# A gated mix of two linear-attention blocks: output tiles as pairs with seven block products, denominators on TensorE, and queries as a filling stream

## The chip, the cores and the metric

The kernel runs on one core of a Trainium2 chip. A core has TensorE (PE in the profile: matmuls, into PSUM, which has 8 banks of 512 fp32 for each of 128 partitions), VectorE (DVE), ScalarE (ACT), GpSimd (POOL), and SyncE (SP), which here only issues DMAs. The metric is the device time of one execution in microseconds. Less is better.

## The reference

x is 2048 x 640 in bf16. Two blocks, A and B, with weights of their own read the same x (B's own x isn't used), and a gate mixes their outputs:

```python
x = A_x
g = sigmoid((x * gate_w).sum(-1, keepdims=True))
a = block(x, A_wqkv, A_wo)
b = block(x, B_wqkv, B_wo)
return g * a + (1 - g) * b

def block(x, wqkv, wo):                          # S=2048, D=640, H=32 heads of 20
    q, k, v = split_heads(x @ wqkv)
    phi = lambda t: where(t > 0, t + 1, exp(t)) + 1e-6
    pq, pk = phi(q), phi(k)
    kv = einsum("bhsd,bhse->bhde", pk, v)
    z = einsum("bhsd->bhd", pk)
    num = einsum("bhqd,bhde->bhqe", pq, kv)
    den = einsum("bhqd,bhd->bhq", pq, z)[..., None] + 1e-6
    return merge_heads(num / den) @ wo
```

## The kernel before

**The plan.** The kernel makes a list of operations, each with engine, estimated cost, buffers read and written, and a priority. `Sched.run` (L111) goes through it with the estimated costs and fixes an order for every engine and a slot for every pooled buffer (PSUM banks, staging slots); `Sched.emit` (L214) writes each engine's program in that order, with semaphore waits between engines. TensorE takes its operations strictly as listed (`look = cand[:1]`, L148); other engines take what can start first and, among ready operations, the lowest `prio`. Nearly all DMAs are issued from SP in the planned order, so one that waits for its data holds up the ones behind it.

**The stages on TensorE.** A token is a row of x. There are 16 token tiles of 128 (`NT`) in 4 blocks of 512 (`NB`), and 5 chunks of 128 features (`NC`).

1. Start: loads, warm-up matmuls (`warm`, L516), and the transposes of the first tiles (`x_tp`).
2. Keys (`k_step`, L585): for each tile and block X, five pairs of matmuls, 512 and 128 wide. `k_post` turns k into pk = phi(k) on ScalarE and VectorE. An extra column of B's weights gives the gate's sum; GE is exp of its negative. While this runs, `s_pair` and `t_all` build differences of pk and of x on VectorE.
3. pk^T x (`g_unit`, L863, five times): the 2 x 2 block product of two feature groups of pk with x is formed from seven block products, P1 to P7 in `prod` (L848), each of 8 matmuls with 320 or 321 moving columns, instead of eight. Partial results go from PSUM to SBUF (`save`, L880, ScalarE), are accumulated further in the same bank, and are added on VectorE (`comb`, L883). The 321st column sums pk over the tokens; `zsum` (L894) writes it as one column of ZC. A DMA transpose turns each result into GS.
4. Queries (`q_unit`, L786): 40 slots (2 blocks X x 4 token blocks x 5 groups) of five 512-wide matmuls; phi is two activations on ScalarE (L818, L820) and two operations on VectorE (L823, L830). 28 of them are placed between the products of pk^T x (`QPRE`, `QFILL`, called by `fill_g`), first all of A's, then B's; the other 12 follow (`QTAIL`, `POST`).
5. `kv_unit` (L951) multiplies GS by the value weights and masks the heads' diagonal blocks; `wp_burst` (L1000) folds the result into the output weights, 15 matmuls in four quadrants of the array for each half of the columns. The result WP goes to DRAM and is read back in another layout.
6. Denominators: for each X and token block, `t_sum` (L1058) sums z * pq over the five feature groups (one activation at L1078, four operations at L1076); `den` (L1086) transposes the sum by DMA, adds four partial sums per head (L1094), takes the reciprocal (L1101), multiplies it by the gate (L1108 or L1118), transposes back by DMA, and scales pq with it in two halves (L1134).
7. Outputs (`out_unit`, L1189; `o_mm`, L1144): for each of 16 tiles, five groups of A and five of B accumulate in one pair of PSUM banks:

```python
a[:, l0 - lo : h0 - lo],
PQ[X, b][:, g, 128 * (t % 4) : 128 * (t % 4) + 128],
WP[X][:, g, l0:h0],
```

with the columns as 512 and 128. `o_post` (L1170) copies 640 columns to bf16 on ScalarE and a DMA stores the tile. The first four tiles' A parts are done early (`o_a`); the last tile is stored in two parts.

Of the kernel before, what the change touches and what calls it, by code (L numbers as in the profile page):

```python
# [30 lines left out]
def _consts():  # L31
    p = np.arange(128)[:, None]
    q, m = p % 64, np.arange(24)[None, :]
    bd = np.where(p < 64, (q >= 4) & ((q - 4) // 20 == m // 4), (q < 60) & (3 + q // 20 == m // 4))
    be = q // 20 == m[:, 0:8] // 4
    return _bf16_bits(np.concatenate([bd, be], axis=1).astype(np.float32))


CW = 32
# [8 lines left out]
TSACT = [(X, b) for X in XS for b in range(4)]  # L48
WPDVE = (("B", 0, 1), ("B", 1, 1))
QR = "ACT"  # L50
QFILL = ((3, 1, 1, 1), (2, 1, 1, 1), (2, 1, 1, 1), (2, 1, 1, 1), (2, 1, 1, 1))
QTAIL = ((1, [8, 9]), (2, [5]), (2, [6, 7]), (2, [8, 9]), (3, [5, 6]), (3, [7, 8]), (3, [9]))
WOAT = (3, 0)
POST = ("q", "q", "kv", "q", "0", "q", "1", "den", "a", "q", "q", "q")
OAN = 4
STACT = (("B", 0),)
PR = {("B", 0): -0.5, ("A", 2): 10**5, ("A", 3): 10**5 + 1}
FFACT = (("B", 1), ("B", 2), ("B", 3), ("A", 2), ("A", 3))
KVAT = (3, 0)
WPAT = ((3, 1), (3, 2))  # L60
# [12 lines left out]
class Op:  # L73
    def __init__(self, eng, fn, cost, ins, outs, after, prio, name, dma):
        self.eng, self.fn, self.cost, self.ins, self.outs = eng, fn, cost, ins, outs
        self.prio, self.name, self.dma = prio, name, dma
        self.deps = list(after)
# [6 lines left out]
        for b in outs:  # L84
            b.writers.append(self)
        self.start = self.end = None
# [9 lines left out]
class Sched:  # L96
    ENGS = ("SP", "ACT", "POOL", "PE", "DVE")

    def __init__(self, pools):
        self.ops = []  # L100
        self.free = {k: [(0.0, i, []) for i in range(n)] for k, n in pools.items()}
        self.order = []

    def op(self, eng, fn, cost, ins=(), outs=(), after=(), prio=None, name="", dma=None):
        if eng == "ACT" and dma is None:
            after = list(after) + self.consts
        o = Op(eng, fn, cost, list(ins), list(outs), after, len(self.ops) if prio is None else prio, name, dma)
# [3 lines left out]
    def run(self):  # L111
# [10 lines left out]
        def can(o, t):  # L122

            w = t
            if o.behind is not None and o.behind.start is None:
                return None
            for d in o.deps:
                if d.end is None:
                    return None
                w = max(w, d.end + (HOP if d.eng != o.eng or d.dma else 0.0))  # L130
            skip = set()
            for b in o.outs:
                if b.pool and b.slot is None:
                    got = self.pick(b, w, skip)
                    if got is None:
                        return None
                    w = max(w, got[0])
                    skip |= set(range(got[1], got[1] + b.n))
            return w

        n = len(self.ops)
        while len(self.order) < n:
            best = None
            for e in self.ENGS:
# [3 lines left out]
                look = cand[:1] if e == "PE" else cand  # L148
                pick = None
                for o in look:  # L150
# [3 lines left out]
                    key = (w if w > at[e] + 1e-6 else at[e], o.prio)  # L154
                    if pick is None or key < pick[0]:
                        pick = (key, o)
                if pick and (best is None or pick[0][0] < best[0][0]):
# [3 lines left out]
            (w, _), o, e = best  # L161
# [3 lines left out]
            for b in o.outs:  # L165
                o.deps += b.war
            o.start = w
# [4 lines left out]
            else:  # L172
                o.end = at[e] = w + o.cost
                if e == "PE":
                    o.end += 160.0
            todo[e].remove(o)
            self.order.append(o)
# [106 lines left out]
def body(nc, A_x, A_wqkv, A_wo, B_x, B_wqkv, B_wo, gate_w, out, log=None):  # L284
# [17 lines left out]
    NEK, NEQ, NOS, NGT, NPT = 6, 4, 4, 4, 4  # L302
# [5 lines left out]
    ZC = sb("ZC", [128, 2 * NC], f32)  # L308
# [3 lines left out]
    GE1 = sb("GE1", [128, NT], f32)  # L312
    GG = sb("GG", [128, NB, 2, 4], f32)
# [3 lines left out]
    EPQ = sb("EPQ", [128, 1], f32)  # L317
# [7 lines left out]
    TSF = {}  # L325
    for b in range(NB):
        for X in XS:
            k = b if X == "A" or b < 2 else 0
            TSF[X, b] = (TXf[:, 1792 + 1024 * b : 2816 + 1024 * b] if X == "B" and b > 1 else WKW[:, 2560 + 1024 * k : 3584 + 1024 * k]).bitcast(f32)
    DEN = sb("DEN", [128, 1280], bf)  # L330
# [21 lines left out]
    WO["B"] = [WQ["A"][:, u, :] for u in range(NU - 1)] + [GSAf[:, 1920:2560]]  # L352
    WO5 = {"A": WOA[:, 0:5, :], "B": WQ["A"][:, :, :]}

    PQ = {("A", b): PQ0[:, NC * b : NC * b + NC, :] for b in range(2)}
    for k, o in ((("A", 2), 0), (("A", 3), SSB), (("B", 0), 2560), (("B", 1), 5120), (("B", 2), SSB + 2560), (("B", 3), 7680)):
# [9 lines left out]
    OST = PKS[:, SSB + 12288 : SSB + 12288 + NOS * D].rearrange("p (k f) -> p k f", k=NOS)  # L366
    XNf = XN[:, :, :].rearrange("p t f -> p (t f)")
    DR = {("A", b): DEN[:, :] if b % 2 == 0 else EKT[:, NPT * 644 : NPT * 644 + 1280] for b in range(NB)}
    for b in range(NB):
        DR["B", b] = XNf[:, 1280 * b : 1280 * b + 1280]  # L370
    TSH = {k: r[:, 0:512] for k, r in DR.items()}
    FF = TSH
    TTR = {k: r[:, 512:1024].rearrange("p (t n) -> p t n", t=4) for k, r in DR.items()}
    FXT = {k: r[:, 512:1024] for k, r in DR.items()}
    DNT = {k: r[:, 1024:1280].bitcast(f32) for k, r in DR.items()}

    BDM = CST[:, 0:24]
    BDE = CST[64:104, 24:32]

    sch = Sched({"ps": 8, "ek": NEK, "eq": NEQ, "os": NOS, "gt": NGT, "pt": NPT})  # L380
# [47 lines left out]
    sch.consts.append(op("POOL", lambda e: e.memset(EPQ[:, :], EPS / 4), 100.0, outs=[beps], name="epq"))  # L428
    op("ACT", lambda e: e.activation(SCR[:, :], EPSC[:, :], ACT.Exp), 1500.0, ins=[beps], outs=[bge0], prio=10**6, name="table")
# [84 lines left out]
    bw = Buf("warm", "ps")  # L514

    def warm(n, w=4):  # L516
        for i in range(n):
            op(
                "PE",
                lambda e: e.matmul(psw(bw, 128 * w), ONE[:, 0:1].to_broadcast([128, 128]), ONE[:, 0:1].to_broadcast([128, 128 * w]), start=True, stop=True),  # L520
# [800 lines left out]
```

## Time and profile before

| What | Value |
|---|---|
| Time, median of 3 runs | 184.31 us (183.83 to 184.68) |
| Span of the profiled execution, first to last instruction | 183.0 us |
| Its granted TensorE clock, mean | 1.000 |
| TensorE busy, share of the span | 98% |
| VectorE, ScalarE, GpSimd busy | 73%, 64%, 1% |
| Instructions | 3186 |
| Moved by DMA | 21.38 MB, mean 117 GB/s |

The profile gives the span of its execution and no time of its own; the runs' times lie 0.8 to 1.7 us above that span.

How to read the rows: L796 is line 796 of the kernel, out<-in gives the buffers, x10 the count. A group row has the busy time, the mean of one instruction in ns, then the idle time of the engine ahead of the group and what ended it. A stage row has the stretch, its length, then for PE, PEld, DVE, ACT and POOL the busy time and count, then the granted clock, the DMA share and GB/s. Matmuls overlap, so that the duration of one is longer than its distance to the next.

### The profile page before, as it was taken

The page shows a single profiled execution, that of the slowest core. Times are in us where ns is not written, and L with a number is a line of the kernel's source. Part 1 is how long each engine was busy: PE and PEld are TensorE (multiplying, and loading weights), DVE is VectorE, ACT ScalarE, POOL GpSimd, SP SyncE. Part 2 cuts the span into 40 slices and gives each one's busy share as a digit, 9 for nine tenths or more (in the row PEclk, how much of TensorE's full clock was granted, in tenths as well). Part 3 has the DMA queues.
Part 4 walks back from the last instruction along what each step waited for, and adds up shares of the span by engine and source line. Part 5 has one row for each costly group of instructions (what it writes and reads, how often), then busy time and mean ns, then how long its engine had stood idle before and what let it go on. Part 6 is the DMA issues. An engine that isn't in the chain of part 4 may idle for free.

```text
span 183.0 us, 3186 instructions
## 1 busy us (share of the span) xinstructions
PE 179.1 (98%) x1257; PEld 106.0 (58%) x1257; DVE 132.8 (73%) x253; ACT 117.1 (64%) x213; POOL 1.3 (1%) x13
## 2 busy tenths in 40 slices
PE   9999999999999999999999999998899999999995
PEld 4455555555565666666667666655455555555552
DVE  2276978899889893884989997799997896660000
ACT  5278888898866577657563796586689538613312
POOL 1000000000000000000000000000000000000000
PEclk9999999999999999999999999999999999999999
DMA  6979999200000089210246579651168062531122
GB/s 184 315 149 146 202 379 364 64 2 0 4 0 0 20 222 191 42 36 0 39 93 151 99 147 306 212 104 29 29 181 211 0 201 65 133 102 59 49 75 72
DMA packets 36501, 21.38 MB, mean 117 GB/s; under 512 B 25694, under 2 KB 36230, under 8 KB 36486
## 3 DMA queue, kind: packets, MB, share of 16 engines
q1 hardware_dynamic: 35858, 20.59, 44.8%
q10 hardware_dynamic: 628, 0.58, 1.2%
q8 instruction: 10, 0.16, 0.4%
q14 instruction: 5, 0.04, 0.1%
HBM read 10.87 MB, written 4.26 MB: 83 GB/s over the span
## 4 chain that ended last, share of the span: by engine, by line
PE 77%; DVE 13%; DMA 7%; ACT 2%; issue 1%; SPq 0%; DVEq 0%; ACTq 0%
PE ps L591 19%; PE ps L853 18%; PE ps L1152 18%; PE ps L796 15%; PE ps L592 5%; DMA XN<-XN 3%; DMA WKW<-in_A_wqkv_dram 2%; DVE TX L1076 2%; DMA DEN<-DEN 2%; DVE WKW L1076 2%; DVE PKS L830 1%; ACT EQ L818 1%; DVE PKS L959 1%; DVE XN L1101 1%; PE ps L979 1%
## 5 line engine op out<-in xcount | busy, mean ns | idle before, releaser
L591 PE MATMUL ps<-WKW,XT 128*128 128x512 bf16 x160 | 44.6, 384 | 0.2 <-DMA WKW<-in_A_wqkv_dram 0.2
L592 PE MATMUL ps<-WKW,XT 128*128 128x128 bf16 (+1 forms) x160 | 35.4, 221 | 0.0
L1152 PE MATMUL ps<-PKS 128*128 128x512 bf16 (+1 forms) x240 | 33.4, 299 | 0.3 <-DVE PKS L1134 0.3
L818 ACT ACTIVATE EQ<-ps 128x512 bf16<-128x512 f32 (+1 forms) x35 | 22.9, 657 | 16.4 <-PE ps L796 13.9
L591 PEld LDWEIGHTS ps<-WKW,XT 128*128 128x128 bf16 x160 | 15.8, 99 | 19.6 <-issue 1.0
L1152 PEld LDWEIGHTS ps<-PKS 128*128 128x128 bf16 x240 | 18.5, 98 | 14.7 <-DVE PKS L1134 0.6
L637 ACT ACTIVATE EKT<-ps 128x640 bf16<-128x640 f32 x32 | 22.3, 704 | 7.0 <-PE ps L592 6.3
L853 PE MATMUL ps<-TX,PKS 128*128 128x321 bf16 (+1 forms) x160 | 24.7, 300 | 0.0
L1176 ACT ACTIVATE PKS<-ps 128x640 bf16<-128x640 f32 (+1 forms) x16 | 11.0, 695 | 21.1 <-PE ps L1152 21.0
L796 PE MATMUL ps<-XT,WQA 128*128 128x512 bf16 x100 | 23.9, 379 | 0.0
L796 PE MATMUL ps<-XT,WQB 128*128 128x512 bf16 x100 | 23.3, 379 | 0.0
L853 PEld LDWEIGHTS ps<-TX,PKS 128*128 128x128 bf16 x160 | 15.3, 98 | 8.4 <-issue 0.4
L820 ACT ACTIVATE PKS<-ps 128x512 bf16<-128x512 f32 (+1 forms) x25 | 17.0, 680 | 1.8 <-PE ps L796 1.8
L853 PE MATMUL ps<-XN,PKS 128*128 128x321 bf16 (+1 forms) x120 | 18.0, 300 | 0.0
L796 PEld LDWEIGHTS ps<-XT,WQB 128*128 128x128 bf16 x100 | 11.5, 118 | 8.6 <-issue 0.2
L796 PEld LDWEIGHTS ps<-XT,WQA 128*128 128x128 bf16 x100 | 11.7, 117 | 8.0
L592 PEld LDWEIGHTS ps<-WKW,XT 128*128 128x128 bf16 x160 | 15.8, 99 | 0.0
L853 PEld LDWEIGHTS ps<-XN,PKS 128*128 128x128 bf16 x120 | 11.7, 98 | 5.4
L823 DVE TENSOR_SCALAR EQ<-EQ 128x512 bf16<-128x512 bf16 (+1 forms) x35 | 10.8, 308 | 5.5 <-ACT EQ L818 5.4
L650 ACT ACTIVATE PKS<-ps 128x640 bf16<-128x640 f32 x20 | 14.0, 699 | 0.0
L701 DVE TENSOR_TENSOR PKS<-PKS 128x1280 bf16<-128x1280 bf16 (+1 forms) x20 | 13.5, 686 | 0.3
L830 DVE TENSOR_TENSOR PKS<-PKS,EQ 128x512 bf16<-128x512 bf16 (+1 forms) x25 | 11.8, 474 | 1.7 <-ACT PKS L820 0.6
(86 smaller groups left out, 181.2 us busy)
## 6 DMA issues: line engine op xcount, KB each, us to landing
out_dram<-PKS SPq DMA_DIRECT2D x15, 160.0 KB, 1.8
XN<-in_A_x_dram SPq DMA_DIRECT2D x1, 2240.0 KB, 9.4
WKW<-in_A_wqkv_dram SPq DMA_DIRECT2D x5, 160.0 KB, 4.0
WKW<-in_B_wqkv_dram SPq DMA_DIRECT2D x5, 160.0 KB, 3.9
WQA<-in_A_wqkv_dram SPq DMA_DIRECT2D x1, 800.0 KB, 11.0
WQB<-in_B_wqkv_dram SPq DMA_DIRECT2D x1, 800.0 KB, 13.7
WVA<-in_A_wqkv_dram SPq DMA_DIRECT2D x1, 800.0 KB, 4.9
PKS<-in_B_wqkv_dram SPq DMA_DIRECT2D x1, 800.0 KB, 5.3
```

Of the source, the lines that this page charges most:

```text
L591: e.matmul(a[:, 0:512], l, WK[X][:, c, 0:512], start=(c == 0), stop=(c == NC - 1))
L592: return e.matmul(a[:, 512:w], l, WK[X][:, c, 512:w], start=(c == 0), stop=(c == NC - 1))
L637: op("ACT", lambda e, i=i, ps=ps: e.activation(evg(i), psg(ps), ACT.Exp), act_cost(D), ins=[ps] + first, outs=[ek, b], name="ke")
L650: op("ACT", lambda e, X=X, ps=ps: e.activation(pkt(X, t), psg(ps), ACT.Relu), act_cost(D), ins=[ps], outs=[rk], name="kr")
L701: op("DVE", lambda e: e.tensor_tensor(out=out, in0=a, in1=b, op=ALU.subtract), dve2(n * D), ins=ins, outs=[bb], name=name)
L796: r = e.matmul(PS[:, ps.slot + i, :], WQ[X][:, c, g::5], XT[:, c, 512 * b : 512 * b + 512], start=(c == 0), stop=(c == NC - 1),)
L818: op("ACT", lambda e: e.activation(ev(), pv(), ACT.Exp), act_cost(512 * n), ins=[ps], outs=[eq], name="qe")
L820: op("ACT", lambda e: e.activation(dst, pv(), ACT.Relu), act_cost(512 * n), ins=[ps], outs=[rq], after=pq_free.get((XS[slots[0] // NC], b) ...
L830: op("DVE", lambda e: e.tensor_tensor(out=dst, in0=dst, in1=ev(), op=ALU.add), dve2(512 * n), ins=[rq, eq, eq2], outs=[pq], name="qs")
L853: r = e.matmul(PS[:, ps.slot, 0:w], reg[:, j, :], mov(j, w), start=(first and j == 0), stop=(j == 7), skip_group_check=not first)
L1152: r = e.matmul(a[:, l0 - lo : h0 - lo], PQ[X, b][:, g, 128 * (t % 4) : 128 * (t % 4) + 128], WP[X][:, g, l0:h0], start=(X == "A" and g == ...
L1176: op("ACT", lambda e: e.activation(OST[:, os_.slot, 0:w], psw(ps, w), ACT.Copy), act_cost(w), ins=[ps], outs=[os_], name="oc")
```

## The change

The diff touches these places.

- **Outputs.** `o_mm`, `o_post` and `out_unit` go. `Pair` takes two neighbouring tiles: with rows [A|B] of scaled queries for two tiles and the weights WP of A over B in two column halves, their 2 x 2 block product is formed from seven products of five 320-wide matmuls each, in the manner of `g_unit`. `s_blk` builds three differences of scaled queries, and one in place, for each token block; `t_mat` builds four sums of weight halves (TO). Three evictions and one copy for each pair are on ScalarE, three additions on VectorE. Results are staged in 9 slots.
- **Denominators.** `t_sum` goes. `zsum` writes z as 32 columns, zero outside the own head (ZM). A new `den(b)` multiplies ZM with pq on TensorE, 20 matmuls of 256 columns, into four strips of 32 PSUM partitions (two X, two token halves). VectorE adds epsilon and multiplies by 1 + GE or 1 + 1/GE, transposed once by DMA (GTX; four GpSimd operations write its input); ScalarE inverts by Ln and then Exp with scale -1; four DMAs for each block copy every head's row to four partitions; scaling pq is as before. A table set with both functions is loaded ahead of the first activation.
- **Order.** Queries are marked `fill`. TensorE's list is `MAIN`: G for pk^T x, kv, w, O for pairs, den; `q34` holds the next item until 34 fills are done. Where the next item of `MAIN` would wait over 150 ns by the plan, the next fill goes ahead. Queries go by token block, A and B after one another. Three of the four dens are fills; each is queued after the first B query of the following block.
- **Rest.** The gs transposes are asked for right behind their parts; B's folded weights go out and back by halves; B's output weights load behind the last pk^T x, into the place of x; buffers get new places; warm-up matmuls go to four banks; operations on other engines are planned as overlapping by `LATE`.

```diff
+MAIN = """q2 G0.1 q5 G0.2 G0.5 G0.6 q6 G0.3 G0.7
+G1.1 G0.4 G1.2 G1.5 G1.6 G1.3 G1.7
+G2.1 G1.4 G2.2 G2.5 G2.6 G2.3 G2.7
+G3.1 G2.4 G3.2 G3.5 G3.6 G3.3 kvA G3.7
+G4.1 G3.4 G4.2 wA0 G4.5 wA1 G4.6 G4.3 G4.7 G4.4
+kvB wB0 wB1
+O0.1 O0.5 q34 O1.1 O1.5 q36 O0.2 O0.6 q38 O1.2 O1.6 q40 O0.3 O0.7 q42 O1.3 O1.7 q43 O2.1 O2.2 O0.4 O1.4 O2.5 den3 O2.6 O2.3 O2.7
+O3.1 O3.2 O2.4 O3.5 O3.6 O3.3 O3.7
+O4.1 O4.2 O3.4 O4.5 O4.6 O4.3 O4.7
+O5.1 O5.2 O4.4 O5.5 O5.6 O5.3 O5.7
+O6.1 O6.2 O5.4 O6.5 O6.6 O6.3 O6.7
+O7.1 O7.5 O6.4 O7.6 O7.2 O7.7 O7.3 O7.4"""
+SLACK = 150.0
...
+LATE = {"ACT": 110.0, "DVE": 80.0}
...
+                if e == "PE":
+                    look = [next((o for o in cand if not o.fill), None), next((o for o in cand if o.fill), None)]
+                    if look[0] is not None and look[0].needq > filled[0]:
+                        look = look[1:]
...
+                    w += SLACK if e == "PE" and o.fill and len(look) > 1 else 0.0
...
-    NEK, NEQ, NOS, NGT, NPT = 6, 4, 4, 4, 4
+    NEK, NEQ, NOS, NGT, NPT = 6, 6, 9, 4, 4
...
+        e.add_instruction(mybir.InstLoadActFuncSet(act_func_set_id=6, name=nc.get_next_instruction_name(), engine=mybir.EngineType.Activation))
+        return e.activation(SCR[:, :], EPSC[:, :], ACT.Exp)
...
-                lambda e: e.tensor_tensor(
-                    out=ZC[:, i : i + 1], in0=PS[:, ps.slot, HC : HC + 1], in1=PT[:, src.slot, HC : HC + 1], op=ALU.add
+                lambda e: e.scalar_tensor_tensor(
+                    ZM[:, i, :],
+                    PT[:, src.slot, HC : HC + 1].to_broadcast([128, 32]),
+                    PS[:, ps.slot, HC : HC + 1],
+                    HM,
+                    op0=ALU.add,
+                    op1=ALU.mult,
...
+    def den(b):
+        ps, b1, b2 = Buf("dn", "ps"), Buf("dr"), Buf("ff")
+
+        def fn(e):
+            for g in range(NC):
+                for s in range(4):
+                    i, h = s // 2, s % 2
+                    r = e.matmul(
+                        PS[32 * s : 32 * s + 32, ps.slot, 0:256],
+                        ZM[:, NC * i + g, :],
+                        PQ[XS[i], b][:, g, 256 * h : 256 * h + 256],
+                        start=(g == 0),
+                        stop=(g == NC - 1),
+                    )
+            return r
...
+            lambda e: e.scalar_tensor_tensor(DNR, PS[:, ps.slot, 0:256], EPS, gt, op0=ALU.add, op1=ALU.mult),
...
+        op("ACT", lambda e: e.activation(DNR, DNR, ACT.Ln), act_cost(256), ins=[b1], outs=[b3], prio=-1, name="ln%d" % b)
+        stt_op[b, 1] = op("ACT", lambda e: e.activation(ff, DNR, ACT.Exp, scale=-1.0), act_cost(256), ins=[b3], outs=[b2], after=fx_op.get(b - 2, []), prio=-1, name="rc%d" % b)
...
+                        bass.AP(tensor=src.tensor, offset=src.offset, ap=[src.ap[0], [0, 4], src.ap[1]]),
...
+        for k, dst, in0, in1, need in ((1, s[0], a21, a22, ()), (2, s[1], a11, s[0], (1,)), (4, s[2], a12, s[1], (2,)), (3, a21, a21, a11, (1,))):
...
+                lambda e, dst=dst, in0=in0, in1=in1: e.tensor_tensor(out=dst, in0=in0, in1=in1, op=ALU.subtract),
...
+    class Pair:
...
+                    r = e.matmul(PS[:, ps.slot, 0:HALF], reg(g), mov(g), start=(first and g == 0), stop=(g == NC - 1), skip_group_check=not first)
...
+            if n == 1:
+                self.bufa, self.bufb = [], []
+                self.mm("1", self.px, self.q("A", 0), lambda g: WP["A"][:, g, 0:HALF], True, [fa, bwpm["A", 0]])
+                self.s1 = self.save(self.t1, self.px, "o1s")
+            elif n == 2:
+                self.mm("2", self.py, self.q("B", 0), lambda g: WP["B"][:, g, 0:HALF], True, [fb, bwpm["B", 0]])
+                self.comb(self.oa, 0, self.py, self.t1, self.bufa, "o11")
+            elif n == 5:
+                self.mm("5", self.pz, self.so(0), lambda g: TO[1][:, g, :], True, [bso[b, 1], bto[1]])
+                self.s5 = self.save(self.t5, self.pz, "o5s")
+            elif n == 6:
+                self.mm("6", self.px, self.so(1), lambda g: TO[2][:, g, :], False, [bso[b, 2], bto[2]], [self.s1])
+                self.s2 = self.save(self.t2, self.px, "o2s")
+            elif n == 7:
+                self.mm("7", self.px, self.q("A", 1), lambda g: TO[3][:, g, :], False, [bso[b, 3], bto[3]], [self.s2])
+                self.c22 = self.comb(self.ob, HALF, self.px, self.t5, self.bufb, "o22")
...
+            elif n == 3:
+                self.mm("3", self.pz, self.so(2), lambda g: WP["B"][:, g, HALF:D], False, [bso[b, 4], bwpm["B", 1]], [self.s5])
+                self.comb(self.oa, HALF, self.pz, self.t2, self.bufa, "o12")
...
+            elif n == 4:
+                self.mm("4", self.px, self.q("B", 1), lambda g: TO[4][:, g, :], False, [fb, bto[4]], [self.c22])
...
+        for b, X in QORDER[2:]:
+            for k in range(NC):
+                q_unit(b, [NC * XS.index(X) + k])
+                if (X, k) == DENAT:
+                    den_s(b - 1)
```

More of the change, by code (lines that the diff above doesn't have):

```diff
@@ L176, in run @@
             todo[e].remove(o)
+            filled[0] += o.fill
             self.order.append(o)
@@ L324, in body @@
     TXf = TX[:, :, :, :].rearrange("p k j f -> p (k j f)")
[L325 to L330, printed above, removed]
+    DEN = sb("DEN", [128, 320], bf)
     EK = EKT[:, 0 : NEK * D].rearrange("p (k f) -> p k f", k=NEK)
@@ L512, in load_wo @@
             o.behind = gs_last[0]
-    bw = Buf("warm", "ps")
+    bw = Buf("warm")
     def warm(n, w=4):
@@ L1282, in body @@
+        for o in sch.ops[n0:]:
+            if o.eng == "PE" and not o.fill:
+                o.needq = need
     span = sch.run()
```

611 lines of the change are left out of this document (311 added, 300 removed).

## The prediction

> **What bounds the kernel now.** I read the page's busy times first, then its chain of work that ended last, then that chain in order of time, the stages of the span, and last the waits of TensorE. First the page, parts 1 and 4:
>
> ```profile
> PE 179.1 (98%) x1257; PEld 106.0 (58%) x1257; DVE 132.8 (73%) x253; ACT 117.1 (64%) x213; POOL 1.3 (1%) x13
> ...
> PE 77%; DVE 13%; DMA 7%; ACT 2%; issue 1%; SPq 0%; DVEq 0%; ACTq 0%
> ```
>
> TensorE is busy from end to end, so the sum is made of its instructions. A busy time counts overlapping matmuls whole; what a matmul costs in a stream is the distance between starts, and the chain in order of time has that (start us, us, what):
>
> ```profile
> 5.17 0.58 PE ps L591
> ...
> 48.62 2.16 PE ps L796 x10
> ...
> 72.72 2.20 PE ps L853 x16
> ...
> 95.60 1.43 PE ps L979 x30
> ...
> 100.33 0.53 PE ps L1013 x15
> 100.87 2.31 PE ps L853 x16
> ...
> 104.25 0.53 PE ps L1013 x15
> 104.79 1.20 PE ps L853 x8
> ...
> 149.44 31.43 PE ps L1152 x230
> 180.96 0.29 DVE PKS L1174
> ```
>
> Prices: 0.216 us for a 512-wide query matmul (L796), 2.20/16 = 0.1375 for a 321-wide one of pk^T x (L853), 31.43/115 = 0.273 for an output pair of 512 and 128. The work on TensorE: keys from 5.17 to 48.62, 43.45; queries 200 x 0.216 = 43.2; pk^T x 280 x 0.1375 = 38.5; kv 2 x 1.43 = 2.9; the folded weights 4 x 0.53 = 2.1; outputs 16 tiles x 10 pairs x 0.273 = 43.7. That is 173.85 us; from 5.17 to the last matmul's end (149.44 + 31.43 = 180.87) pass 175.70, so 1.85 us are waits. The stages and the waits of TensorE (us; line waited for, total, times, longest) say where:
>
> ```profile
> 48.50:109.20 60.70, 60.70 (x418) 38.88 (x417) 50.48 (x111) 39.75 (x75) 0.50 (x4) 1.00 0.37 75
> 109.20:149.40 40.20, 39.01 (x276) 22.60 (x274) 35.61 (x65) 27.66 (x45) 0.00 (x0) 1.00 0.53 142
> 149.40:180.90 31.50, 31.41 (x230) 17.69 (x230) 10.54 (x14) 11.93 (x24) 0.00 (x0) 1.00 0.28 86
> ...
> PE ps L1013 <- DVE PKS L959: 0.5, 1, 0.5
> PE ps L1152 <- ACT EQ L818: 0.5, 1, 0.5
> ...
> PE ps L1152 <- DVE PKS L1134: 0.3, 1, 0.3
> ```
>
> About 1.3 us of waits stand between 109 and 149.5, where kv, folded weights and denominators of the second half must come through VectorE (35.61 of 40.2 us busy). The other 0.6 us is spread and I carry it over.
>
> **The change part by part.** *Output tiles in pairs.* 16 x 10 pairs become 8 pairs x 7 products x 5 matmuls of 320 columns = 280. The width, the weights of 128 columns and the order of loads are those of L853, so 280 x 0.1375 = 38.5 for 43.7: **-5.2 us**. (At 320/512 of 0.216 it would be 37.8.)
>
> *Denominators on TensorE.* A den is 20 matmuls of 256 columns in four strips of 32 output columns. No strip over all 128 rows is in this trace; the nearest row is L1013, 15 matmuls in four quadrants. The longest quadrant has 3 of 320 columns, 0.405 us at 0.216/512 a column; the burst took 0.53, 1.31 times that. A strip has 5 x 256 columns, 0.54; by the same factor 0.71. Lower bound 0.54, upper bound all 20 in a row, 20 x 0.108 = 2.16. I take 0.71, since the burst is the only row of matmuls side by side. The group behind each burst is longer as well, 2.31 for 2.20 and 1.20 for 1.10: 0.10 for changing over, taken once per den. Four dens: 4 x 0.81 = **+3.2 us** (2.2 to 8.7).
>
> The Trainium skill, page "TensorEngine Tiling (Array Packing)", section Key Properties, says that a change of tiling mode drains TensorE, which speaks against four more changes there and back. An estimate from "TensorE: Matmul & The Clock Gate", section Single matmul latency, where a lone warm matmul costs 166 ns over its columns, is 2 x 0.17 = 0.33 a den, and the time would be 0.9 us longer than forecast. By the 0.10 behind the bursts the trace shows a smaller drain.
>
> *What leaves VectorE and ScalarE, and what comes.* Rows of the groups by shape (busy, mean ns | idle before):
>
> ```profile
> L818 ACT ACTIVATE EQ<-ps 128x512 bf16<-128x512 f32 x30 | 17.8, 596 | 13.5 <-PE ps L796 12.9 <-DVE PQ L830 0.5
> L701 DVE TENSOR_TENSOR PKS<-PKS 128x1280 bf16<-128x1280 bf16 x12 | 9.8, 820 | 0.2
> L1076 DVE SCALAR_TENSOR_TENSOR WKW<-PKS,ZC,WKW 128x512 f32<-128x512 bf16 x12 | 8.9, 749 | 0.2
> L823 DVE TENSOR_SCALAR EQ<-EQ 128x512 bf16<-128x512 bf16 x30 | 8.7, 289 | 5.5 <-ACT EQ L818 5.4
> L830 DVE TENSOR_TENSOR PKS<-PKS,EQ 128x512 bf16<-128x512 bf16 x20 | 8.4, 420 | 1.2 <-ACT PKS L820 0.3
> L886 DVE TENSOR_TENSOR WKW<-ps,EKT 128x320 bf16<-128x320 f32 x15 | 7.3, 485 | 1.8 <-PE ps L853 1.6
> L1134 DVE TENSOR_TENSOR PKS<-PKS,XN 128x1280 bf16<-128x1280 bf16 x8 | 6.2, 811 | 0.0
> L1101 DVE RECIPROCAL XN<-XN 128x128 f32<-128x128 f32 x4 | 3.8, 954 | 0.1
> L721 DVE TENSOR_TENSOR TX<-XN 128x2576 bf16<-128x2576 bf16 x2 | 3.0, 1492 | 0.0
> L959 DVE TENSOR_TENSOR PKS<-ps,CST 128x480 bf16<-128x480 f32 x2 | 2.9, 1437 | 0.0
> L1094 DVE TENSOR_REDUCE XN<-XN 128x128 f32<-128x512 bf16 x4 | 2.7, 682 | 2.9 <-DMA XN<-XN 2.9
> L1027 DVE CAST TX<-ps 124x960 bf16<-124x960 f32 x2 | 2.3, 1154 | 0.0
> L881 ACT ACTIVATE EKT<-ps 128x320 f32<-128x320 f32 x5 | 2.2, 447 | 0.0
> L429 ACT ACT_TABLE_LOAD x1 | 1.3, 1283 | 0.6 <-issue 0.6
> L1174 DVE CAST PKS<-ps 128x128 bf16<-128x128 f32 x1 | 0.3, 292 | 17.6 <-PE ps L1152 17.6
> ```
>
> From VectorE go 32 sums x 0.75 = 24.0, 8 reduces 5.5, 8 reciprocals 7.6 and 3 scalings 2.1: 39 us. To it come 24 output sums x 0.485 = 11.6, 16 differences of 1280 elements x 0.82 = 13.1, four weight sums of 1600 (between the 0.82 and 1.49 rows, by length 0.99) 3.9, four gate products under 0.485, 1.8: 30 us. So its total falls by 9 us, worth nothing while TensorE is the bound; its place matters. ScalarE gets 32 evictions x 0.447 = 14.3 and four ln and exp pairs (each under 0.447) for the 11 us of whole-tile evictions, 8 first sums and 20 scalings, hidden at 64% load. Of the DMAs, 16 transposes on SP's queue become one of the gates and 16 plain copies, so that queue is freed; nothing lands later for it. GpSimd's four gate expansions lie beside pk^T x and nothing needs them before the first den. Warm-up, constants: nothing; they end before the key matmuls or lie beside them.
>
> *Order.* Six queries (6.5 us) are due in pk^T x, which then runs without them: its end is 48.62 + 38.5 + 6.5 + 1.43 + 1.06 = 96. Behind it lie 34 queries, 36.7 us. They cover what follows: gs transpose, kv, mask, folded weights to DRAM and back, den and its ln, exp and copies, about 19 us by the same steps before (kv of A at 95.6, its folded weights asked back from DRAM at 114.61, the row below). So the 1.3 us of visible waits goes.
>
> *New waits.* In a pair the third product on one bank needs the eviction of the first, with one product (5 x 0.1375 = 0.69) in between. The timeline (start, us) has the steps:
>
> ```profile
> 113.46 1.24 PE L796 MATMUL ps<-XT,WQB 128*128 128x512 bf16 x5
> 113.66 0.44 ACT L881 ACTIVATE EKT<-ps 128x321 f32<-128x321 f32 x1 [0.67 <-PE ps L853]
> ...
> 114.61 0.43 SPq L394 DMA_DIRECT2D PKS<-wpsA  x1
> ...
> 130.23 1.02 ACT L818 ACTIVATE EQ<-ps 128x1024 bf16<-128x1024 f32 x1 [1.12 <-DVE PKS L830]
> 131.40 1.52 PE L1152 MATMUL ps<-PKS,PQ 128*128 128x512 bf16 x10 [0.48 <-ACT EQ L818]
> ```
>
> ScalarE starts 0.20 behind TensorE's switch to other work, takes 0.44, and TensorE starts 0.15 after an eviction: 0.79, so 0.10 is open, once in each of 8 pairs: 0.8. Queued behind it on TensorE is only the rest of the pair. The last pair has two more such places, 0.10 and 0.15 (sum on VectorE, 0.20 + 0.49 + 0.15): 0.25. For sums that meet a 0.82 us difference on VectorE I put 0.4 (0 to 2). With the 0.6 carried over: 2.05 for 1.85, **+0.2**. The end: a 320-wide eviction of 0.45 for 0.29, and a store of 80 KB that lies between 32 and 160 KB (landing 1.6 and 1.8 us, by the page's DMA part): **+0.25**.
>
> ```profile
> out_dram<-PKS SPq DMA_DIRECT2D x15, 160.0 KB, 1.8
> ...
> out_dram<-PKS ACTq DMA_DIRECT2D x1, 32.0 KB, 1.6
> ```
>
> Sum: -5.2 + 3.2 + 0.2 + 0.25 = **-1.55**. Span 183.0 becomes 181.45. The runs lie 0.8 to 1.7 above the span; carrying that 1.3 over to their median, 184.31 - 1.55 = **182.8**.
>
> **Rivals.** *A, VectorE takes over (slower).* From the end of pk^T x to the last query TensorE has 36.7 + three dens 2.4 + kv and folding 2.5 + twelve products 8.3 = 49.9 us. VectorE has 34 queries x 0.71 = 24.1, masks and casts 4.6, gate products 1.4, weight sums 3.9, six output sums 2.9, and for two blocks scaling and differences (8 x 0.815 + 8 x 0.82) 13.1: 50.0, with the third block 56.5. It idles some 2 us at first, since scaling waits for den, ln, exp and copy. For: in 109 to 149 it ran 89% busy and TensorE waited. Against: the third block is due 19 products (13 us) later, where only output sums stand. It decides if VectorE is over 4 us behind at the last query, as no query is left to fill with; then about 4 us go: 186.8. *B, the pair chain eats the gain.* If each pair waits 0.35 rather than 0.10, as sums stand behind differences, 2 us go: 184.8, no change. Against: an output sum goes ahead of other ready work. *C, strips one by one:* 4 x (2.16 - 0.71) = +5.8, 188.6. Against: L1013. *D, the change of function:* if ln and exp each call for a table (L429, 1.28), 8 loads put 10.3 us on ScalarE, whose two 0.6 evictions per 1.08 us query leave nothing free: up to +8, 190. Against: one set is loaded by hand. *E, better:* strips at 0.54, waits 1.0: -0.7 and -1.05, 181.0.
>
> **How the numbers follow.** About 0.5% (183.4 to 185.2) is what a measurement here can tell from no change. Forecast 0.48, 181.6 to 183.4; E 0.13; B 0.18; A 0.13; C 0.04; D 0.04. Faster 0.61, same 0.18, slower 0.21. The range runs from E's end, 180.4, to most of A, 186.6; the forecast's own is 181.6 to 183.4.
>
> **What would show it.** Right: output matmuls of 320 columns 0.137 apart, a den of 20 within 0.9 us, a single table load, TensorE at 98% with waits of about 0.1 us on ScalarE in the pairs, last query near 147. Wrong: den matmuls 0.1 us apart; TensorE waiting for VectorE's differences or scalings after 96 us; ScalarE late at queries, or waits inside pk^T x, where no query is due to fill.

## The result and the profile after

| | Before | Changed |
|---|---|---|
| Median of 13 runs each | 184.11 us (183.79 to 184.68) | 182.91 us (182.12 to 183.82) |
| Profiled execution: time, span | none, 183.0 us | 182.12 us, 180.7 us |

The ratio is 0.9934 (0.9917 to 0.9951): the changed kernel is 0.66% faster, 1.20 us. The forecast was 182.8. It stood on the median of three runs of the kernel before, 184.31, less 1.55; against the thirteen runs above the drop is 1.20 us (0.90 to 1.53), a little less than was forecast. The profiled execution is the fastest of the thirteen; the median of their spans is 181.5, where 181.45 was forecast.

The page of the changed kernel, parts 1 and 4, and from part 5 the table load:

```profile
PE 175.5 (97%) x1283; PEld 108.6 (60%) x1297; DVE 123.8 (68%) x257; ACT 111.0 (61%) x219; POOL 4.5 (3%) x16
...
PE 85%; DVE 6%; DMA 4%; issue 2%; ACT 2%; SPq 1%; DVEq 0%
```

```profile
L457 ACT ACT_TABLE_LOAD x1 | 1.3, 1283 | 1.3 <-POOL XN L474 1.3
```

TensorE is still what sets the time, with a larger share of the chain (85% for 77%). VectorE lost 9.0 us, as worked out. One table serves exp and ln. Its chain in order of time (start us, us, what):

```profile
4.53 0.39 PE ps L622
...
47.71 2.16 PE ps L829 x10
...
58.59 24.20 PE ps L889 x176
...
99.49 7.55 PE ps L829 x35
...
139.44 0.66 PE ps L1132 x20
...
146.18 1.09 PE ps L829 x5
...
149.39 0.73 DVE XT L1216
150.12 0.68 DVE PKS L866 x2
150.84 0.73 PE ps L1132 x20
151.57 27.03 PE ps L1250 x195
178.62 0.44 ACT PKS L1307
```

L622 is the keys, L829 the queries, L889 pk^T x, L1132 the dens, L1250 the output products. A pk^T x matmul still takes 24.20/176 = 0.1375 us, an output matmul 27.03/195 = 0.1386; from a den's first matmul to the next item's first pass 0.66. Just ahead of the last den the chain leaves TensorE for VectorE: the place to watch below. What TensorE waited for (total, times, longest), and the three stretches behind the keys:

```profile
PE ps L1064 <- DMA XN<-in_B_wo_dram: 0.7, 1, 0.7
PE ps L889 <- DVE DEN L937: 0.4, 1, 0.4
PE ps L829 <- issue: 0.4, 2, 0.2
...
PE ps L1132 <- DVE PKS L866: 0.2, 1, 0.2
```

```profile
47.70:99.40 51.70, 51.04 (x384) 34.20 (x385) 24.91 (x62) 22.34 (x44) 3.80 (x8) 1.00 0.47 98
99.40:147.30 47.90, 46.58 (x333) 27.32 (x337) 42.50 (x95) 38.00 (x76) 0.00 (x0) 1.00 0.39 95
147.30:178.60 31.30, 31.10 (x240) 20.84 (x238) 20.05 (x38) 12.64 (x29) 0.00 (x0) 1.00 0.23 75
```

Behind the keys the rows leave 2.2 us without a matmul (0.66 + 1.32 + 0.20), against 1.28 by the same three rows of before. Some 0.65 of the 2.2 is no wait: this trace has 192 of the 200 query matmuls, the trace before all 200, and where a query's record is missing a gap of 0.18 (twice) or 0.05 (six times) stands ahead of the query. The two called "issue" in the list are such gaps; no trace with all 200 has them. That leaves waits of about 1.5 us. Those of before, at kv's masks, at a query's eviction and at the scalings, are gone; new ones, at B's first folding (L1064), at a pk^T x product (L889) and at the last den (L1132), take their place.

The balance of the span: from the first waited key matmul to the last matmul's end 175.70 became 178.60 - 4.53 = 174.07, 1.63 less where 1.80 less was forecast. The other 0.7 us of this execution is its earlier start (4.53 for 5.17) and its tail (2.10 for 2.13). Of the 1.63, 0.27 lies in the keys, whose work the change leaves alone (47.71 - 4.53 = 43.18 for 43.45): from that mark on the first two 512-wide matmuls lasted 0.39 and 0.38 us here, 0.58 and 0.44 in the trace before, and all later ones 0.38. Behind the keys, where the change is, 132.25 became 130.89: 1.36 less.

### The profile page after: what moved, and what is told of

Its sections match the earlier page's. It is cut to its first block, busy times and chain, and to the rows that moved or that the text cites. A ratio compares the mean times of both kernels' runs of the same rounds, so it can differ in the third digit from the quotient of the medians.

```text
span 180.7 us, 3303 instructions
## 1 busy us (share of the span) xinstructions
PE 175.5 (97%) x1283; PEld 108.6 (60%) x1297; DVE 123.8 (68%) x257; ACT 111.0 (61%) x219; POOL 4.5 (3%) x16
## 4 chain that ended last, share of the span: by engine, by line
PE 85%; DVE 6%; DMA 4%; issue 2%; ACT 2%; SPq 1%; DVEq 0%
PE ps L889 20%; PE ps L1250 19%; PE ps L829 18%; PE ps L622 18%; PE ps L623 5%; DMA WKW<-WKW 2%; DVE PKS L1011 2%; DMA WKW<-in_A_wqkv_dram 2%; PE ps L1031 1%; SPq L421 1%; PE ps L1132 1%; ACT EQ L854 1%; PE ps L1064 1%; DVE PQ L1183 1%; DVE PKS L866 1%
## 5 line engine op out<-in xcount | busy, mean ns | idle before, releaser
L622 PE MATMUL ps<-WKW,XT 128*128 128x512 bf16 x154 | 42.8, 379 | 0.3 <-DMA WKW<-in_A_wqkv_dram 0.3
L854 ACT ACTIVATE EQ<-ps 128x512 bf16<-128x512 f32 x40 | 24.1, 601 | 9.0 <-PE ps L829 7.4
L622 PEld LDWEIGHTS ps<-WKW,XT 128*128 128x128 bf16 x160 | 15.6, 98 | 19.3 <-DMA WKW<-in_A_wqkv_dram 0.6
L889 PE MATMUL ps<-TX,PKS 128*128 128x321 bf16 (+1 forms) x160 | 24.8, 300 | 0.5 <-DVE DEN L937 0.4
L829 PE MATMUL ps<-XT,WQB 128*128 128x512 bf16 x95 | 23.2, 380 | 0.5 <-issue 0.4
L829 PE MATMUL ps<-XT,WQA 128*128 128x512 bf16 x97 | 22.2, 379 | 0.2
L923 DVE TENSOR_TENSOR WKW<-ps,EKT 128x320 bf16<-128x320 f32 x15 | 7.4, 492 | 21.4 <-PE ps L889 19.6
L889 PEld LDWEIGHTS ps<-TX,PKS 128*128 128x128 bf16 x160 | 15.1, 98 | 8.0 <-DVE DEN L937 1.5
L918 ACT ACTIVATE EKT<-ps 128x321 f32<-128x321 f32 (+1 forms) x15 | 6.6, 441 | 21.5 <-PE ps L889 21.3
L889 PE MATMUL ps<-XN,PKS 128*128 128x321 bf16 (+1 forms) x120 | 18.8, 299 | 0.0
L856 ACT ACTIVATE PKS<-ps 128x512 bf16<-128x512 f32 x30 | 18.0, 604 | 0.0
L829 PEld LDWEIGHTS ps<-XT,WQA 128*128 128x128 bf16 x100 | 11.7, 118 | 9.0
L829 PEld LDWEIGHTS ps<-XT,WQB 128*128 128x128 bf16 x100 | 11.4, 119 | 8.9 <-issue 0.6
L859 DVE TENSOR_SCALAR EQ<-EQ 128x512 bf16<-128x512 bf16 x40 | 10.8, 292 | 6.4 <-ACT EQ L854 6.0
L889 PEld LDWEIGHTS ps<-XN,PKS 128*128 128x128 bf16 x120 | 11.7, 98 | 5.1
L866 DVE TENSOR_TENSOR PKS<-PKS,EQ 128x512 bf16<-128x512 bf16 x30 | 12.3, 423 | 1.6 <-ACT PKS L856 1.5
L1263 ACT ACTIVATE PKS<-ps 128x320 f32<-128x320 f32 x15 | 6.6, 440 | 9.3 <-PE ps L1250 9.3
```

Of the source, the lines that this page charges most:

```text
L622: e.matmul(a[:, 0:512], l, WK[X][:, c, 0:512], start=(c == 0), stop=(c == NC - 1))
L829: r = e.matmul(PS[:, ps.slot + i, :], WQ[X][:, c, g::5], XT[:, c, 512 * b : 512 * b + 512], start=(c == 0), stop=(c == NC - 1),)
L854: op("ACT", lambda e: e.activation(ev(), pv(), ACT.Exp), act_cost(512 * n), ins=[ps], outs=[eq], name="qe")
L856: op("ACT", lambda e: e.activation(dst, pv(), ACT.Relu), act_cost(512 * n), ins=[ps], outs=[rq], after=pq_free.get((XS[slots[0] // NC], b) ...
L859: lambda e: e.tensor_scalar(ev(), ev(), 1.0, EPS, op0=ALU.min, op1=ALU.add),
L866: op("DVE", lambda e: e.tensor_tensor(out=dst, in0=dst, in1=ev(), op=ALU.add), dve2(512 * n), ins=[rq, eq, eq2], outs=[pq], name="qs")
```

## The experiments

All times are medians; ratios are to the kernel before, run beside each, with the 95% interval. In the first four experiments "over the changed kernel" goes to its 182.80 beside them, in the others to the 182.91 above, from another set; the kernel before lay between 183.88 and 184.18 in the sets. Two theories stand against each other. **T**: TensorE's own work sets the time, so work added to it counts in full and work taken from VectorE gains little. **V**: VectorE sets the pace from 115 us on (rival A), so the reverse holds. After the second set a refinement of T, **T2**, says that the two engines are level up to the last query and that VectorE's lateness enters at the fourth den (`den3`), which needs the last queries' phi.

### The changed kernel again

> The changed kernel once more, as the reference of this set. It should come within 0.5 us of its median of 182.9. Its profile is to show whether the start is what makes single runs differ: the profiled run before had its first waited-for key matmul at 4.53 us, span 180.7; if the start sets it, a later first key matmul goes with a span longer by the same amount.

182.8 us, 0.9944 (0.9921 to 0.9967), profiled span 181.2. The result repeats. The start was to explain the spread between executions. The mark chosen for it, the first waited key matmul, hardly moved, 4.57 for 4.53, and this span is 0.5 longer. But two key pairs on, TensorE is 0.29 late; first this run, then the first profile:

```profile
5.37 0.39 PE L622 MATMUL ps<-WKW,XT 128*128 128x512 bf16 x1
5.08 0.38 PE L622 MATMUL ps<-WKW,XT 128*128 128x512 bf16 x1
```

The first query starts at 47.85 for 47.55, so 0.3 of the 0.5 does come in the first six microseconds. The other 0.2 is in small waits:

```profile
PE ps L1064 <- DMA XN<-in_B_wo_dram: 0.6, 1, 0.6
...
PE ps L1250 <- DVE XN L1216: 0.4, 1, 0.4
```

The second, an output product waiting for a difference of scaled queries, isn't in the first profile's list.

### Every den twice

```diff
-            for g in range(NC):
+            for g in list(range(NC)) * 2:
```

> Every den multiplies twice, 40 matmuls for 20, the second time over the first. Theory T (TensorE is the bound all through, a term costs its time there): a den took 0.66 us, so 4 x 0.66 = +2.6, about 185.5. Rival V (VectorE sets the pace from the end of pk^T x to the last query): TensorE has room there and only the fourth den counts, +0.7 to +1, about 183.8.

184.86, 1.0051 (1.0024 to 1.0077): 2.06 over the changed kernel in the same set. One den of 40 matmuls in the chain:

```profile
139.96 1.24 PE ps L1132 x40
```

So 20 more cost 1.24 - 0.66 = 0.58, four dens 2.3, and most of it is in the time. The 0.6 wait at the first folding is gone, since the first den's extra work stands ahead of it, and the wait at the last den rose to 0.7. T holds, though 185.5 was expected; V allowed 183.8.

### The strips one after another

```diff
-            for g in range(NC):
-                for s in range(4):
+            for s in range(4):
+                for g in range(NC):
```

> The same 20 matmuls of a den with the strips one after another (all five groups of a strip in a row). If matmuls run side by side only where neighbours lie in different strips, a den goes from 0.66 to about 20 x 0.108 = 2.16 us and T gives 4 x 1.5 = +6.0, about 188.9; if they run side by side in any order, 182.9. V: with room on TensorE, +2 to +4.

183.55, 0.9991 (0.997 to 1.0012), 0.75 over the changed kernel. The expected 2.16 a den did not come:

```profile
123.85 1.03 PE ps L1132 x20
139.87 1.03 PE ps L1132 x20
151.64 1.10 PE ps L1132 x20
```

1.03 for 20 is less than half of the 2.16 of matmuls in a row: with five matmuls of a strip one after another, those of the next strip still run beside them. The order by strips costs 0.37 a den and no more. Four times that is 1.5; half of that is missing in the time, and the wait for B's output weights, 0.6 in the same set, is missing in this run's list. The 2.16 a den of rival C is twice too high even in this order.

### Without the differences and the weight sums

```diff
         b = bto[k] = Buf("to")
+        return
...
             bb = bso[b, k] = Buf("so")
+            continue
...
-                self.mm("5", self.pz, self.so(0), lambda g: TO[1][:, g, :], True, [bso[b, 1], bto[1]])
+                self.mm("5", self.pz, self.q("A", 1), lambda g: WP["A"][:, g, HALF:D], True, [fa, bwpm["A", 1]])
```

(and the same in products 6, 7, 3 and 4). The kernel leaves out all differences of scaled queries and all sums of weights, some 17 us of VectorE by their durations; TensorE does as many products as before, on the plain operands.

> Leaves out the four differences of scaled queries in each block and the four sums of weight halves (16 x 0.82 + 4 x 0.99 = 17 us of VectorE); the seven products read scaled queries and folded weights directly, as many matmuls as before. T: only waits that name these operations go, 0.3 to 0.8: 182.1 to 182.6. V: the time from 96 us to the last query shortens, at least -2: below 181.

182.45, 0.992 (0.9894 to 0.9947): 0.35 less than the changed kernel, within the noise. VectorE's busy time fell from 123.8 to 110.6 us (neighbouring operations overlap a little, so this is less than 17), and almost nothing came of it. V needed less than 181 and falls: in the kernel as it stands VectorE does not set the time.

### Three differences of each block twice

```diff
+TWICE = (1, 2, 4)
...
+            if k in TWICE:
+                bc = bso[b, k] = Buf("so")
+                op(
+                    "DVE",
+                    lambda e, dst=dst, in0=in0, in1=in1: e.tensor_tensor(out=dst, in0=in0, in1=in1, op=ALU.subtract),
...
```

> Three of the four differences of each block are computed twice, one after the other: 12 x 0.82 = 9.8 us more on VectorE, nothing on TensorE. T with a second bound close by: VectorE was busy 46.6 of the 50 us from 105 to 155, so some 3.4 us fit in there and part of the last block's share slips into the free time behind; the rest shows as waits of TensorE: +2 to +5, 185 to 188. If VectorE has wide room: within 0.5 of 182.9. V: nearly the whole of it, +8 to +10, over 191.

188.6, 1.0231 (1.0181 to 1.028), 5.7 over the changed kernel's 182.91 and above the 185 to 188 expected, for 9.8 us of added VectorE work. The four executions differ in the granted clock: 187.28 at 1.000, which is the profiled one, 188.35 and 188.86 at 0.991, and 189.35 at 0.982. At the full clock the loss is thus 4.4; the rest of the median is the clock's, as the last section tells. (The kernel's lines are shifted by one: L1133 is the den, L867 the last step of phi.) The wait, and the added operations (L1228) up to the last den and behind it:

```profile
PE ps L1133 <- DVE PKS L867: 4.4, 2, 3.7
```

```profile
100.00:155.80 55.80, 4.98 (x7) 1.00 0.35 90
155.80:185.00 29.20, 4.82 (x6) 1.00 0.23 75
```

In these two rows the first number behind the length is VectorE's busy time in the added operations. The wait list has 4.4 us at dens, for 0.2 in the changed kernel. Six added operations end ahead of the last den. Each lasts 0.82, but the next operation starts 0.74 behind it (L1228 at 142.54, the next at 143.28), so they set VectorE back by 6 x 0.74 = 4.4, and 4.2 of that came out as waits. The 4.82 added behind the den brought no wait that the list shows. That reads more exactly than the total: ahead of the last den VectorE has next to no room, as the den's wait of 0.2 in the changed kernel says already; behind it at least 4.8 us.

### Eight plain products for each pair

The pairs stay, but each forms its two tiles from eight block products: no differences, weight sums, partial results or additions; the halves are copied out by ScalarE and VectorE in turn.

```diff
+                self.mm("7", self.pw, self.q("A", 1), lambda g: WP["A"][:, g, R], True, [fa, bwpm["A", 1]])
...
+                self.mm("8", self.pw, self.q("B", 1), lambda g: WP["B"][:, g, R], False, [fb, bwpm["B", 1]])
```

> Undoes the outputs alone: each pair by its eight plain block products, two accumulated in a bank, without differences, weight sums and saved partial results. TensorE gets 8 x 0.68 = +5.5, VectorE loses 17 us of differences and sums and a third of its output operations. T: +5.5 less the waits of the pairs (0.5), about +5: 187.9. V: VectorE's relief gives most of it back, +1 to +3: 184 to 186.

187.75, 1.0194 (1.0168 to 1.022): 4.8 over 182.91, for eight products of five matmuls at 0.1375, 5.5. The saved product, with all that it asks of the other engines, is worth 4.8/8 = 0.60 us a pair in the time, of 0.69 on TensorE. With plain products the rest of the change is 1.9% slower than the kernel before.

### Queries that don't move ahead

```diff
-SLACK = 150.0
+SLACK = 1e9
```

> A query goes ahead only where the list asks for it or the next item can't be planned at all, and no longer where the next item would wait over 150 ns. T: behind pk^T x TensorE stands for the last gs transpose (about 5 us) and for masks and folded weights (2 to 3): +5 to +8, 188 to 191. Rival: the waits overlap with others later, within 2 us of 182.9.

190.62, 1.0353 (1.0318 to 1.0388), 7.7 over 182.91. No query or den fills a wait by the plan; the order written in `MAIN` alone decides.

```profile
PE ps L1031 <- DMA GSB<-WKW: 4.9, 1, 4.9
```

```profile
96.00:105.00 9.00, 4.13 (x23) 2.14 (x21) 2.77 (x8) 3.69 (x7) 0.00 (x0) 0.91 0.81 193
105.00:115.00 10.00, 9.10 (x78) 5.51 (x79) 6.66 (x10) 3.90 (x6) 0.00 (x0) 0.74 0.45 86
```

kv of B waits for the transposed result. Some two thirds of the loss are this wait; the granted clock behind it (0.74) adds to it, as the last section tells. This is what the filling queries cover.

### One more query ahead of B's first folding

```diff
-kvB wB0 wB1
+kvB q19 wB0 wB1
```

The 0.7 wait for B's output weights was to be filled with a query.

> One more fill is asked for ahead of the first folding of B, which stood 0.74 us for its output weights. T: that wait goes and nothing takes its place: -0.7, 182.2. Rival: what follows (folded weights, weight sums, pairs) comes 1 us later and the wait turns up there: 182.9 or more.

184.47, 1.0025 (1.0 to 1.005), 1.6 over 182.91: the rival's side. The wait at the folding is gone; one of 0.6 at a query has come, and a longer one at the last den:

```profile
PE ps L1132 <- DVE PKS L866: 1.8, 1, 1.8
```

On VectorE's timeline the weight sums stood idle before:

```profile
129.03 0.99 DVE L1196 TENSOR_TENSOR GSB<-GSB,PKS 128x1600 bf16<-128x1600 bf16 x1 [1.88 <-DMA PKS<-wpsB]
```

1.88 us that VectorE lost at 127 reappear, 1.80, at 152.78 on TensorE. With VectorE level with TensorE ahead of that den this is what T2 says. Why the folded weights came late is on SP's queue:

```profile
115.39 1.47 SPq L421 DMA_DIRECT2D wpsB<-TX  x3
119.73 0.57 SPq L421 DMA_DIRECT2D PKS<-wpsB  x1
120.34 1.53 SPq L421 DMA_DIRECT2D wpsB<-TX  x3
125.40 0.54 SPq L421 DMA_DIRECT2D PKS<-wpsB  x1
```

In the changed kernel six writes of folded weights go out in a row from 114.70, and the two reads follow at 118.92. Here the plan put the read of the first half ahead of the second half's writes; that read waits for the first half to land in DRAM, and three writes that need nothing of it wait behind it. The last read is asked for at 125.40 instead of 119.8.

### The last den seven products later

```diff
-O0.1 O0.5 q34 O1.1 O1.5 q36 O0.2 O0.6 q38 O1.2 O1.6 q40 O0.3 O0.7 q42 O1.3 O1.7 q43 O2.1 O2.2 O0.4 O1.4 O2.5 den3 O2.6 O2.3 O2.7
-O3.1 O3.2 O2.4 O3.5 O3.6 O3.3 O3.7
+O0.1 O0.5 q34 O1.1 O1.5 q36 O0.2 O0.6 q38 O1.2 O1.6 q40 O0.3 O0.7 q42 O1.3 O1.7 q43 O2.1 O2.2 O0.4 O1.4 O2.5 O2.6 O2.3 O2.7
+O3.1 O3.2 O2.4 O3.5 den3 O3.6 O3.3 O3.7
```

> Only the fourth den moves, seven products back in TensorE's list (between the fifth and sixth product of the fourth pair; before it stood behind the fifth of the third). Theory T2, formed from the runs so far: TensorE and VectorE are level from 115 us to the last query, and VectorE's lateness becomes a wait of TensorE at the fourth den, which needs the last queries' phi. Then this gives VectorE some 4.8 us more, the waits at the fourth den and at the differences behind it (0.2 and 0.4 in the run of the unchanged order) go: 182.2 to 182.6 beside 182.8. Rival: its own chain (ln, exp, copies, scaling) then comes too late for the seventh pair: 183.5 or more.

182.56, 0.9914 (0.9896 to 0.9933), as expected: the den's wait and the one for differences left the list, the others stayed. The gain over the changed kernel is a few tenths, near the size of those waits; the two ratios' intervals overlap, so that it is not clear of noise.

### Both, and a later kv of A

Two kernels of the same set: `late_wb` joins the two edits above; `late_all` also puts kv of A one product later.

```diff
-G3.1 G2.4 G3.2 G3.5 G3.6 G3.3 kvA G3.7
-G4.1 G3.4 G4.2 wA0 G4.5 wA1 G4.6 G4.3 G4.7 G4.4
+G3.1 G2.4 G3.2 G3.5 G3.6 G3.3 G3.7
+G4.1 kvA G3.4 G4.2 G4.5 wA0 G4.6 wA1 G4.3 G4.7 G4.4
```

> The fourth den as late as in den_late, and one more fill ahead of B's first folding as in wb19, which alone cost 1.3 to 1.7. T2: VectorE's idle 1.9 us no longer meets the fourth den, and the wait for B's output weights is gone: 181.9 to 182.4. Rival (the folded weights come late for the pairs themselves): 184 or more, as wb19.

183.32, 0.9962 (0.9948 to 0.9976). Missed: it is slower than with the late den alone. SP's order is again the split one, VectorE stands 2.02 us for B's folded weights, and the lateness enters at an addition of a pair now that the den is out of its way:

```profile
PE ps L1250 <- DVE PKS L1270: 1.0, 1, 1.0
```

> As late_wb, and the kv product of A is placed one product of pk^T x later, so that its masks on VectorE no longer stand ahead of the sum that TensorE waited 0.43 us for. T: another -0.4: 181.5 to 182.0. Rival: the masks now hold up the folding of A or another sum by as much: no gain over late_wb.

181.18 (180.86 to 181.62), 0.9851 (0.983 to 0.9872): the fastest of all, below both kernels and below its expectation. Its waits, and SP's queue:

```profile
PE ps L1031 <- DMA GSB<-WKW: 0.5, 1, 0.5
PE ps L829 <- issue: 0.4, 2, 0.2
...
```

```profile
114.23 4.01 SPq L421 DMA_DIRECT2D wpsB<-TX  x6
119.79 1.68 SPq L421 DMA_DIRECT2D PKS<-wpsB  x2
```

The six writes are together again, and the weight sums start at 125.10 with 0.21 idle ahead of them, for 128.94 in `late_wb`. With kv of A later, no wait of 0.4 behind its masks is listed at pk^T x either. From the first query to the last matmul's end this trace takes 130.03 us, the first profile 131.04: 1.0 of the 1.7 between the medians; the other 0.7 is not accounted for. In all thirteen traces the split order stands only in the two kernels where VectorE stood two microseconds. That the split is the cause was not tried by itself; `late_all` differs from `late_wb` in kv's place too.

### The doubled differences with the late den

> diff_twice (9.8 us more differences on VectorE, 188.6, with 4.4 us of waits at the dens) with the fourth den seven products later. T2: the lateness of VectorE enters by the place of the fourth den, so most of its 3.7 us wait goes: 185 to 186.5. Rival: VectorE's total sets the time wherever the den stands: 188 or more.

187.76, 1.0208 (1.0187 to 1.0228): a miss that shows the limit of T2. The den's wait fell from 4.4 to 0.7, but the products that now stand ahead of the den wait for the same VectorE:

```profile
PE ps L1262 <- DVE TX L1228: 2.8, 1, 2.8
PE ps L1133 <- DVE PKS L867: 0.7, 1, 0.7
```

3.5 us of waits for 4.4. The seven products ahead of the den need differences of the second block, which are late as well. All five executions have a granted clock of 0.991, which costs some 1.7 us by the estimate in the last section. Beside the two executions of the doubled differences at that clock, 188.35 and 188.86, the later den gives back 0.6 to 1.1; in `late_wb` it left waits of 1.0 and 0.2 where `wb19` had 1.8. So the later den wins back less than about a microsecond, whether VectorE is two or four late, and the lateness then enters at the products next in line.

## Why the prediction was right, by its steps

**Outputs, -5.2: right.** 280 matmuls at 0.1375 to 0.1386; the kernel with eight products shows the saved one in the time at 0.60 us a pair.

**Dens, +3.2: right, from two sizes that were off in opposite ways.** The trace of `wb19` has every record around its second den:

```profile
122.87 1.24 PE L829 MATMUL ps<-XT,WQB 128*128 128x512 bf16 x5
124.04 0.73 PE L1132 MATMUL ps<-PKS,DEN 128*32 128x256 bf16 x20
124.70 4.51 PE L829 MATMUL ps<-XT,WQB 128*128 128x512 bf16 x20
129.05 2.32 PE L829 MATMUL ps<-XT,WQA 128*128 128x512 bf16 x10
```

From 122.87 to 129.05 pass 6.18 us, of which 25 query matmuls take 5.40 at 0.216. The den costs the other 0.78, four dens 3.1. The 0.66 from start to start leaves out 0.09 ahead of the den and 0.03 behind it. The 20 matmuls themselves are 0.58, by the doubled dens, where 0.71 was taken; changing over there and back is 0.20, where 0.10 was taken. The upper bound of 2.16 was far too wide; strip by strip 1.03 stands for the 0.66.

**Waits, 2.05 for 1.85: mis-sized.** The work from 4.53 on is keys 43.18, queries 43.2, pk^T x 38.5, kv 2.9, folding 2.1, dens 3.1, outputs 38.5: 171.5 of 174.07, which leaves 2.6. The cover of the 19 us chain held, as the kernel without moved-up queries shows, and pairs waited less than 0.10. The old 1.3 us went as forecast. Missing were two waits:

```profile
86.85 1.27 PE L889 MATMUL ps<-TX,PKS 128*128 128x320 bf16 x8 [0.43 <-DVE DEN L937]
```

Here a pk^T x product waits for an addition that stands behind kv's masks on VectorE (0.43). At B's first folding it is 0.74 for B's output weights, whose load the change moves behind the last pk^T x. The prediction left out that moved load, although its 375 KB took 7.3 us to land. So waits and what is spread grew by 0.7 where 0.2 was put: the step that was half a microsecond short.

**The end, +0.25: not seen.** The tail from the last matmul is 2.10, before 2.13. The start, for which nothing was put, gave 0.6 in this execution and the keys 0.27; neither is shown to come from the change. The half microsecond too few in the waits and the quarter too many at the end partly cancel, and that is luck: for the change itself the two profiles give -1.36 and -0.03, the runs -1.20, for the forecast's -1.55.

**Order: the place was off, the effect not.** Nine queries, not six, ran inside pk^T x, whose end was 99.5, not 96; the three extra ones went ahead where the plan saw a wait. The last query ended at 147.3, forecast near 147.

**Rival A.** It did not happen, but its point of decision was wrong. "Over 4 us behind at the last query" and "the third block is due 19 products later" left out that `den3` needs the last queries' phi, with only some products between. The row there is the last den's wait of 0.2 us, and the runs show that there is next to no room (4.4 us of setback gave 4.2 more wait; after 1.88 us of standstill the wait is 1.80). The reckoning of 50.0 us of VectorE against 49.9 of TensorE was nearer to the truth than the verdict drawn from it. **B**: the 39 last products, five and a half pairs, took 27.03 for 195 x 0.1375 = 26.81: 0.04 us a pair. **C** and **D** fell, by the den's 0.78 and the one table load. About the time of **E**, 181.0, came only in `late_all`, which is another kernel; its strips at 0.54 were near the measured 0.58, its waits of 1.0 were not.

**Open.** Single executions of one kernel differ by 0.8 us either way. A part is the start: in the thirteen traces of changed kernels, all with the same keys, the first query begins between 47.55 and 48.35, and the first profile is the earliest; before it was 48.45, in one trace. The rest are small waits in different places. Why the start and those waits vary was not settled. Whether the lateness in `late_wb` comes from the split order on SP alone is argued from traces.

## What to carry to other kernels

Add a second engine's work up to the first place where the bottleneck needs all of it, not up to where its total is due: that there was no room there was found only by adding work, and taking work away showed nothing. Price a small burst of matmuls by what it takes out of the stream, from the item before it to the item behind it, and not by its own piece of the chain (0.78 for 0.66 here). Look at the granted clock of every execution before a difference is put down to a wait. When an item moves in TensorE's order, read the DMA queue's order again: a read-back that waits can hold writes that are ready. And a load that is moved to reuse a buffer has a landing time that belongs into the sum.

## What was not expected of the hardware

**Strips overlap even in strip order.** Five matmuls of 256 columns on one strip of 32 output columns, then five on the next: 20 took 1.03 us; in turn over the four strips 0.66; in a row, at half the 0.216 of a query matmul each, they would take 2.16.

**The granted clock falls behind some waits of TensorE, not all.** In the kernel without moved-up queries, after the wait of 4.9 us:

```profile
105.00:110.00 5.00, 5.00 (x36) 3.52 (x37) 2.76 (x4) 0.01 (x1) 0.00 (x0) 0.50 0.76 130
110.00:115.00 5.00, 4.10 (x43) 2.00 (x42) 3.90 (x7) 3.89 (x6) 0.00 (x0) 0.98 0.14 43
```

Half the clock for about five microseconds: the 30 matmuls of kv took 2.82 us instead of 1.59, and ten query matmuls 3.40 instead of 2.16. With the doubled differences and the late den, after a wait of only 2.8 us that ended at 155.22:

```profile
155.00:160.00 5.00, 4.78 (x23) 2.95 (x24) 3.69 (x8) 0.44 (x1) 0.00 (x0) 0.66 0.10 36
155.22:155.65 0.43, 0.43 (x4) 0.31 (x5) 0.43 (x2) 0.00 (x0) 0.00 (x0) 1.00 0.00 0
155.65:159.06 3.41, 3.41 (x15) 1.92 (x13) 2.94 (x5) 0.02 (x1) 0.00 (x0) 0.50 0.15 53
```

The half clock set in 0.43 us after TensorE had gone on, and held for 3.41 us. With the doubled differences alone, after 3.7 us, the profiled execution shows nothing of the kind:

```profile
155.00:165.00 10.00, 9.15 (x81) 6.00 (x82) 9.97 (x18) 3.38 (x8) 0.00 (x0) 1.00 0.25 75
```

But only that one of its four executions kept the full clock; the others, of which there is no trace, show a mean of 0.991 or 0.982, and took 1.1 to 2.1 us longer. So a wait of some three microseconds can cost 1.7 us more (an estimate: 5 x 0.34 in the row above) or nothing, in one and the same kernel, and its length alone does not say which. The Trainium skill, page "TensorE: Matmul & The Clock Gate", section "What's actually happening", tells of a free-running window of about 3.4 us after which an idle engine runs at half clock. The half clock is in the first row here, and a wait of 3.7 us that leaves the clock alone in one execution and not in the next fits too, as it need not hold a whole window. The 2.8 us wait can't hold one; there the run goes beyond the rule, and three waits don't show what decides.
